# Linear attention into a mixture of four experts: another opening, and a bank of its own for the last product

## The chip, the cores and the metric

The kernel runs on one core of a Trainium2 chip. The metric is device time in microseconds, the median of several executions. A second source is one profiled execution, whose trace gives start and duration of every instruction.

## The reference

Two stages, B = 8 batches, H = 8 heads, S = 576 positions, 64 values per head, four experts:

```python
q_p, k_p = phi(q), phi(k)                 # phi(x) = where(x > 0, x, exp(x) - 1) + 1
kv  = einsum('bhsd,bhse->bhde', k_p, v)
z   = k_p.sum(axis=2)
x   = einsum('bhsd,bhde->bhse', q_p, kv) / (einsum('bhsd,bhd->bhs', q_p, z) + 1e-6)
x   = x.transpose(0, 2, 1, 3).reshape(4608, 512)
p   = domain_probs / domain_probs.sum(-1)
out = sum over e of  p[:, e] * (relu(x @ w1[e]) @ w2[e])     # w1: 512x1024, w2: 1024x512
```

## The kernel before

**Tiling.** The attention is done per batch and per pair of heads (four pairs). Of 576 positions, 512 are handled as four chunks of 128, and 64 are a rest. For each pair: phi of k and q (an exponent on ScalarE, ACT, and two operations on VectorE, DVE), a transpose of phi(q) on TensorE (PE), the products kv and z (PE, into PSUM), a copy of kv to SBUF (ACT), numerators and denominators (PE), the division (DVE: a reciprocal and a product). The experts follow on x. Batch 0 is done with plain matrix products (`first_l1`, L775, and `first_l2`, L822); of its 8 column blocks of expert 0, seven are held open at once in seven PSUM banks, so that their four slices of the contraction (dc) can be added as the four pairs of x become ready (L750). Later batches run in 64 units of two chunks and one expert, each with seven products of half size for w1 (`l1_seven`, L897) and seven for w2 (`l2_unit`, L978) in place of eight, with sums of weights (L715, L736) and of activations around them. Four PSUM banks l2b hold the second product over the four experts of a chunk pair.

**Order.** The order of the instructions is set by a planner (class `Plan`, L21): each step is added with an engine, a planned duration, a due time and keys that it reads and writes, and the planner lays them out; every engine then runs its list in that order. The list of POOL (GpSimd), which issues most of the loads up to 68 us, stays in the order in which the steps were added. Between planned steps of the first 21 us, PE runs extra matmuls whose result nobody reads (`keep_warm`, L1161).

**The opening.** `load_first` (L325) loads k, q or v of one pair of batch 0 (256 KB), `load_first_rest` (L333) the rest of k or v of one pair (32 KB), `load_w1` (L348) slices of w1 (512 KB, cast to 16 bits on the way). Before: SP issues k0, q0, k1, two rests of k, four rests of v, q1; ACT issues two rests of k; POOL waits for the landing of k0 (`hold="k0"`) and issues v0, k2, q2, v1, slice 0 of w1, k3, q3, v2, v3, the other slices of w1, and so on (L1090 to L1106, L1110). In `first_attention` (L474) the numerators and denominators of a pair lie side by side, 65 columns a head, two chunks in the bank `at` and two in l2b1 (L511); each half has its own reciprocal (L518) and product (L519); x is transposed (L528) and copied (L533) as the operand of the first product.

**The end.** In the last unit (`end`, L1006) DVE adds up the seven products as they are finished, six additions (L1053), and the result is stored in four parts: the second half of each row block after the fourth addition, the first half after the sixth, one part from SP and one from ACT each time (L1055).

Of the kernel before, what the change touches and what calls it, by code (L numbers as in the profile page):

```python
# [137 lines left out]
def kernel(  # L138
# [16 lines left out]
    P = 128  # L155
# [92 lines left out]
        A["t", 2, i] = [("ek", 2 + i, 0), ("ek", 2 + i, 1)]  # L248
    A["t", 2, 2], A["w1x", 2, 0] = [("k_r", g) for g in range(DC)] + ["v_r", "kp_r"], ["ek_r"] + [("v_r32", g) for g in range(DC)]
    ones = sb("ones", [P, 2, 1], FP16)  # L250
    rc4 = sb("rc4", [P, 2, C], FP32)
    xt0 = s4_b[1].rearrange("p a c t -> p a (c t)")
    hts = [h_b[i][:, t, f].rearrange("p c t -> p (c t)") for i in range(2)
           for t in range(2) for f in range(2)]
# [75 lines left out]
        dma(queue, pri, o, t[0, 2 * pr : 2 * pr + 2, 0:NT].rearrange("h (p c) d -> p h c d", c=C),  # L330
            (key,), 0.72, hold=hold, mark=mark)

    def load_first_rest(t, o, queue, pri, key, g):  # L333

        n = 2 * R // DC
        dma(queue, pri, o[g * n : (g + 1) * n].rearrange("p h t d -> p h (t d)"),
            t[0, 2 * g : 2 * g + 2, NT:S].rearrange("h (p t) d -> p h (t d)", t=2),
            ((key, g),), 0.17)

    def load_rest(b, queue, pri, after=0.0, parts=(0, 1, 2)):  # L340
        par = b % 2
# [132 lines left out]
    def first_attention(pr, pri, step):  # L474
# [3 lines left out]
        fs = slice(pr * P, (pr + 1) * P)  # L478
        g = slice(pr * 2 * R // DC, (pr + 1) * 2 * R // DC)
        ni = pr % 2  # L480
        nds = [bank[:, 0 : C * DE].rearrange("p (c h e) -> p c h e", c=2, h=2)
               for bank in (at, l2b[1])]
        kv3 = l2b[2][:, 0 : 2 * DE].rearrange("p (h e) -> p h e", h=2)
        tq = tbank[:, 0:NT]
        last = pr == DC - 1
# [22 lines left out]
            nc.scalar.copy(kvz[0:D, 0, :], kv3[0:D, 0, :])  # L508
            nc.scalar.copy(kvz[D:P, 1, :], kv3[D:P, 1, :])

        def nd(u):  # L511
            for c in range(2):
                nc.tensor.matmul(out=nds[u][:, c], lhsT=qT[:, 2 * u + c], rhs=kvz,
                                 start=True, stop=True)

        def norm(u):
            rc = rc4[:, u].rearrange("p (c h e) -> p c h e", c=2, e=1)
            nc.vector.reciprocal(rc, nds[u][:, :, :, D:DE])  # L518
            nc.vector.tensor_tensor(  # L519
                out=x_b[0][:, 2 * u : 2 * u + 2, fs].rearrange("p c (h d) -> p c h d", h=2),  # L520
                in0=nds[u][:, :, :, 0:D],
                in1=rc.broadcast_to([P, 2, 2, D]),
                op=AO.mult,
            )

# [17 lines left out]
        pl.add("PE", 0.5, pri + 4 * step, kv,  # L543
               r=(("kqp", pr, 0), ("v_o", pr), "v_r", "kp_r"), w=("l2b2",))
        pl.add("ACT", 0.45, pri + 4.5 * step, kvcopy, r=("l2b2",), w=(("kvz", pr),))
        for u in range(2):
            pl.add("PE", 0.12, pri + (5 + 0.1 * u) * step, lambda u=u: nd(u),
                   r=(("qT", ni), ("kvz", pr)), w=(("at", "l2b1")[u],))
            pl.add("DVE", 0.63, pri + (5.5 + 0.1 * u) * step, lambda u=u: norm(u),
                   r=(("at", "l2b1")[u],), w=(("xk", pr, u),))  # L550
        bk = ("l1b2", "l2b3" if last else "l1b2")
        xw = ("s4", 1, pr)
        for u in range(2):
# [221 lines left out]
    def first_l1(e, pri, step, nb):  # L775
        ht = []
        banks = [(l1b[i], "l1b%d" % i) for i in range(3)]
        if nb > 3:
            banks[2:] = [(l2b[0], "l2b0"), (l2b[2], "l2b2"), (at, "at"), (l2b[1], "l2b1")]
            banks += [(l1b[2], "l1b2")]  # L780
        ht = [rot("ht", len(hts)) for _ in range(FC)]

        def relu(fj, bank, key, pr_):
            if nb > 3 and fj in RELU:
                pl.add("DVE", 0.62, pr_, lambda: nc.vector.tensor_scalar(
                    hts[ht[fj]], bank, 0.0, None, AO.max), r=(key,), w=(HTK[ht[fj]],))
                return
            pl.add("ACT", 0.5, pr_, lambda: nc.scalar.activation(hts[ht[fj]], bank, AF.Relu),
                   r=(key,), w=(HTK[ht[fj]],))

        done = 0
        if nb:
            b0 = cnt.get("l1", 0) if nb < 4 else 0
            late = lambda fj: LATE if fj > 2 else 0.0
# [183 lines left out]
    def l2_unit(n):  # L978
# [5 lines left out]
        KW = lambda i, j_: k2(e, i, j_)  # L984
        T = lambda i: (("t", e, i),)

        def prod(bank, half, a, w, opens):
            for c in range(HF):
                nc.tensor.matmul(  # L989
                    out=l2b[bank][:, half * HD : (half + 1) * HD],  # L990
                    lhsT=a[:, c, :],
                    rhs=w[:, c],
                    start=(opens and first and c == 0),
                    stop=(last and c == HF - 1),
                    skip_group_check=True,
                )

# [8 lines left out]
        end = n == nu - 1  # L1006
        if first:
            seq = (P1, P5, P2, P6, P7, P4, P3)
        elif end:
# [2 lines left out]
        for i, (bank, half, a, ak, w, wk, opens) in enumerate(seq):  # L1012
            pl.add("PE", 0.436, p0 + 0.9 * i,
                   lambda bank=bank, half=half, a=a, w=w, opens=opens: prod(bank, half, a, w, opens),
                   r=(ak,) + wk, w=lk(bank) + ((("p", bank, half),) if end else ()))
        if not last:
            return
        oi = rot("ot", 2)
# [20 lines left out]
        if end:  # L1039
            lo, hi = (lambda bank: l2b[bank][:, 0:HD]), (lambda bank: l2b[bank][:, HD : 2 * HD])  # L1040
            for dur, o, a_, b_, r, w in (
                (0.4, of[:, 0], hi(1), s15[:, 0], (("p", 1, 1), "s15"), (O(0),)),
                (0.4, of[:, 1], hi(0), of[:, 0], (("p", 0, 1),), (O(0),)),
                (0.62, of[:, 2:4], lo(3)[:, None].broadcast_to([P, 2, HD]), of[:, 0:2],
                 (("p", 3, 0), O(0)), (O(2),)),
                (0.4, of[:, 2], hi(2), of[:, 2], (("p", 2, 1),), (O(2),)),
                (0.4, of[:, 0], lo(1), s15[:, 0], ("l2b1",), (O(0),)),
                (0.4, of[:, 1], lo(2), of[:, 1], lk(2), (O(0),)),
            ):
                i = cnt.get("lp", 0)  # L1050
                cnt["lp"] = i + 1
                pl.add("DVE", dur, p0 + 2 + i * 0.5,
                       lambda o=o, a_=a_, b_=b_: tt(out=o, in0=a_, in1=b_, op=AO.add), r=r, w=w)  # L1053
                if i in (3, 5):
                    for par, queue in enumerate(("SP", "ACT")):  # L1055
                        store(int(i == 3), par, queue, (O(2 if i == 3 else 0),))
            return
        pl.add("DVE", 0.62, p0 + 4.5, lambda: tt(
# [16 lines left out]
    def consts(i):  # L1075
# [11 lines left out]
    nc.vector.memset(qTr[0], 0.0)  # L1087
    pl.add("DVE", 0.27, 36, lambda: nc.vector.memset(qTr[1], 0.0),
           w=[("qTr", 1, pr) for pr in range(DC)])
    load_first("SP", -9, k, 0, mark="k0")  # L1090
    load_first("SP", -8, q, 0)
    load_first("SP", -7, k, 1)
    for g in range(DC):
        load_first_rest(k, k_r, "ACT" if g < 2 else "SP", -6, "k_r", g)
    for g in range(DC):
        load_first_rest(v, v_r32, "SP", -4, "v_r32", g)
    load_first("SP", -3, q, 1)
    load_first("POOL", 0, v, 0, hold="k0")
    for pr in (2, 3):
        load_first("POOL", 0, k, pr)  # L1100
        load_first("POOL", 0, q, pr)
        if pr == 2:
            load_first("POOL", 0, v, 1)
            load_w1(0, (0,))
    load_first("POOL", 0, v, 2)
    load_first("POOL", 0, v, 3)  # L1106
    first_rest()
    for pr in range(DC):
# [49 lines left out]
                rest_maps(b, False, t - 2)  # L1158
            attention(b, pr, False, t, 1.5)

    def keep_warm(bank):  # L1161

        nc.tensor.matmul(out=bank[:, 256:512], lhsT=identh,
                         rhs=qTr[0][:, 0:2].rearrange("p a t -> p (a t)"), start=True, stop=True)

    prep(0)
# [11 lines left out]
    with tc.manual_schedule(  # L1178
# [7 lines left out]
    ):  # L1186
        todo = pl.order()
        free = 0.0
        warm, bank = True, l2b[0]
        for o in todo:  # L1190
            warm = warm and not (o["start"] > WARM or "l2b2" in o["w"] and bank is l2b[2] and o["dur"] < 0.3)
            bank = l2b[2] if "l2b0" in o["w"] else bank
            if o["eng"] == "PE" and warm:
                gap = o["start"] - free
                for _ in range(int((gap - 0.25) / 0.115) - (COLD if free == 0.0 else 0)):
                    keep_warm(bank)
                free = o["start"] + o["dur"]
            o["fn"]()

# [29 lines left out]
```

## Time and profile before

| | us |
|---|---|
| median of 4 runs (496.61 to 497.09) | 496.78 |
| profiled execution, device time | 497.0 |
| its span, first to last instruction | 495.2 |
| first L750 (first product of batch 0) starts | 15.37 |
| first L761 (second product of batch 0) starts | 24.80 |
| last matmul ends | 489.6 |
| last of the four last stores lands | 493.8 |

How to read the lines shown further on. The page's first part gives each engine's busy time, its share of the span and its number of instructions; PEld is the loading of weights into PE. A line of the waits has the engine and line that waited, what ended the wait, and total, count and longest in us. A line of the chain has start, duration, engine and what it did; it is the sequence of steps that ended last. A line of the timeline has start and duration (us), engine, line, operation, output and inputs, shape, count, and in brackets the idle time before it and what ended it. SPq, ACTq and POOL with DMA_DIRECT2D are issues of transfers. The DMA view gives the busy share of the 16 DMA engines in tenths and GB/s, in 40 equal slices of its window.

### The profile page before, as it was taken

What the parts mean: (1) busy time and instruction counts of PE and PEld (TensorE: products, weight loads), DVE (VectorE), ACT (ScalarE), POOL (GpSimd) and SP (SyncE); (2) the same over time, 40 slices, a digit from 0 to 9 for tenths busy, and PEclk for the clock granted to TensorE, in tenths of its full rate; (3) what the DMA queues carried; (4) which work ended last, traced back from release to release, by engine and by line L of the source; (5) the groups of instructions that cost most, each with busy time, mean ns of one, the idle gap of its engine ahead of it and who ended that gap; (6) DMA issues with size and microseconds to landing.
All of it is one profiled execution on the core that took longest, in us unless ns stands there. A gap on an engine that the chain in (4) does not pass through costs nothing.

```text
span 495.2 us, 14994 instructions
## 1 busy us (share of the span) xinstructions
PE 484.9 (98%) x6092; PEld 429.9 (87%) x6092; DVE 413.2 (83%) x1045; ACT 364.8 (74%) x686; POOL 41.2 (8%) x66
## 2 busy tenths in 40 slices
PE   7999999999999999999999999999999999999995
PEld 6544557999999999999999999999999999999994
DVE  6798999999998989899989899899987676767664
ACT  5636678978977898769876997699766767676641
POOL 7656600000000000000000000000000000000000
PEclk9999999999999999999999999999999999999998
DMA  8999968946765775878557655655623232323311
GB/s 218 215 233 220 269 140 227 216 88 177 113 164 127 163 157 132 159 159 151 126 128 164 133 151 125 181 126 127 152 54 87 45 87 44 88 44 86 46 44 42
DMA packets 125541, 66.98 MB, mean 135 GB/s; under 512 B 94592, under 2 KB 119696, under 8 KB 125472
## 3 DMA queue, kind: packets, MB, share of 16 engines
q1 hardware_dynamic: 115808, 51.99, 47.2%
q0 software_dynamic: 9344, 13.71, 13.6%
q8 instruction: 47, 0.77, 0.6%
q10 hardware_dynamic: 320, 0.33, 0.2%
q14 instruction: 22, 0.18, 0.1%
HBM read 45.16 MB, written 9.44 MB: 110 GB/s over the span
## 4 chain that ended last, share of the span: by engine, by line
PE 90%; DVE 3%; DMA 3%; ACT 1%; POOL 1%; issue 1%; DVEq 0%; ACTq 0%
PE l1b L913 40%; PE l2b L989 39%; PE l1b L750 4%; PE l2b L761 3%; PE at L653 2%; PE at L629 1%; DMA t<-in_v_dram 1%; DMA xT<-xp 1%; DVE t L736 1%; DMA kq<-in_k_dram 1%; DVE w1x L715 1%; POOL w1x L290 1%; DVE ot L826 1%; ACT xp L873 0%; PE l2b L750 0%
## 5 line engine op out<-in xcount | busy, mean ns | idle before, releaser
L913 PEld LDWEIGHTS <-w 128*128 128x128 f16 x2048 | 134.0, 98 | 5.3
L927 ACT ACTIVATE h<-l1b 128x512 f16<-128x512 f32 x128 | 76.7, 599 | 52.4 <-PE l1b L913 49.9
L989 PE MATMUL l2b<-w,h 128*128 128x256 f16 x768 | 115.0, 273 | 0.0
L989 PE MATMUL l2b<-t,s 128*128 128x256 f16 x768 | 114.6, 273 | 0.0
L913 PEld LDWEIGHTS <-w1x 128*128 128x128 f16 x1536 | 100.2, 98 | 4.1 <-issue 0.6
L989 PEld LDWEIGHTS <-s 128*128 128x128 f16 x1024 | 90.3, 98 | 6.3
L933 DVE CUSTOM_DVE_ANT_0 h<-l1b,p 128x512 f16<-128x512 f32 x64 | 44.2, 690 | 44.2 <-PE l1b L913 41.6
L873 ACT ACTIVATE xp<-x,p_nat 128x512 f16<-128x512 f16 x112 | 77.3, 721 | 2.3 <-DMA xT<-xp 1.9
L913 PE MATMUL l1b<-xs,w1x 128*128 128x128 f16 x1024 | 78.1, 219 | 0.1
L913 PE MATMUL l1b<-xs,w 128*128 128x128 f16 x1024 | 78.0, 219 | 0.0
L913 PE MATMUL l1b<-xT,w 128*128 128x128 f16 x1024 | 78.0, 219 | 0.0
L989 PEld LDWEIGHTS <-h 128*128 128x128 f16 x768 | 67.3, 98 | 4.5
L975 DVE TENSOR_TENSOR s<-h 128x512 f16<-128x512 f16 x128 | 53.9, 421 | 2.1
L930 ACT COPY l1b<-l1b 128x512 f32<-128x512 f32 x64 | 36.8, 574 | 12.0 <-PE l1b L913 11.4
L930 ACT COPY u<-l1b 128x512 f32<-128x512 f32 x64 | 37.5, 585 | 10.8 <-PE l1b L913 10.4
L933 DVE CUSTOM_DVE_ANT_0 h<-l1b,u 128x512 f16<-128x512 f32 x64 | 43.8, 685 | 1.3 <-PE l1b L913 0.2
L930 ACT COPY p<-l1b 128x512 f32<-128x512 f32 x64 | 37.4, 584 | 8.6 <-PE l1b L913 7.6
L891 DVE TENSOR_TENSOR xs<-xT,xs 128x256 f16<-128x256 f16 x128 | 36.9, 288 | 3.5
L913 PE MATMUL l1b<-xT,w1x 128*128 128x128 f16 x512 | 39.0, 219 | 0.0
L989 PE MATMUL l2b<-w,s 128*128 128x256 f16 x256 | 38.4, 273 | 0.0
L594 ACT ACTIVATE ek<-kq 128x512 f16<-128x512 f32 x54 | 33.9, 629 | 2.8 <-DMA kq<-in_k_dram 1.9
L975 DVE TENSOR_TENSOR s<-s,h 128x512 f16<-128x512 f16 x64 | 27.1, 424 | 5.6
(155 smaller groups left out, 579.8 us busy)
## 6 DMA issues: line engine op xcount, KB each, us to landing
w<-in_moe_w_dram POOLq DMA_DIRECT2D x32, 256.0 KB, 8.0
out_dram<-ot SPq DMA_DIRECT2D x16, 512.0 KB, 3.1
kq<-in_k_dram SPq DMA_DIRECT2D x26, 256.0 KB, 3.5
kq<-in_q_dram SPq DMA_DIRECT2D x26, 256.0 KB, 3.4
vs<-in_v_dram SPq DMA_DIRECT2D x24, 256.0 KB, 3.8
xT<-xp SPq DMA_TRANSPOSE x64, 3.1
kq<-in_k_dram POOLq DMA_DIRECT2D x3, 256.0 KB, 7.1
vs<-in_v_dram POOLq DMA_DIRECT2D x3, 256.0 KB, 7.1
```

The source lines that it names most:

```text
L594: pl.add("ACT", 0.55, pri + i * step, lambda i=i: nc.scalar.activation(ek[:, i], kq[:, i], AF.Exp), r=(sk[i],), w=(("ek", ei, i),))
L653: nc.tensor.matmul(out=slot[c - c0], lhsT=qT[:, c] if c < C else qTr[par][:, pr], rhs=kvz, start=True, stop=True,)
L750: nc.tensor.matmul(out=bank[:, ts], lhsT=w1_sb[e][:, dc, fj * P : (fj + 1) * P], rhs=xt0[:, dc, ts], start=(dc == 0), stop=(dc == DC - 1 a ...
L761: nc.tensor.matmul(out=bank, lhsT=hts[ht[fj]][:, c * P : (c + 1) * P], rhs=w2_sb[e][:, fj, :], start=(fj == 0), stop=(fj == FC - 1),)
L873: pl.add("ACT", 0.6, pri, lambda c=c, src=src, ps=ps: nc.scalar.activation(xp[:, c, :], src, AF.Copy, scale=ps), r=r, w=(("xp", xi, c),))
L891: lambda o=o, a=a, b_=b_: tt(out=o, in0=a, in1=b_, op=AO.subtract),
L913: nc.tensor.matmul(out=bank[:, fc * P : (fc + 1) * P], lhsT=wt[:, kc, fc * P : (fc + 1) * P], rhs=r[:, kc, :], start=(start and fc == 0 an ...
L927: return lambda: nc.scalar.activation(o, bank, AF.Relu)
L930: return lambda: nc.scalar.copy(o, bank)
L933: return lambda: nc.vector._custom_dve(TENSOR_ADD_SAT, out=o, in0=bank, in1=t, s0=BIG, s1=0.0)
L975: pl.add("DVE", 0.36, U(n + 1) + d - 0.5, lambda i=i, a=a, b_=b_, alu=alu: tt(out=s4[:, i], in0=a, in1=b_, op=alu), r=r, w=(Q(i),))
L989: nc.tensor.matmul(out=l2b[bank][:, half * HD : (half + 1) * HD], lhsT=a[:, c, :], rhs=w[:, c], start=(opens and first and c == 0), stop=( ...
```

## The change

Five edits.

1. *Loads.* SP issues k0, q0, k1, q1 and then the rests of v. ACT issues all four rests of k, the first of which is now what POOL's first load waits for. POOL issues v0, k2, q2, v1, k3, q3, v2, slice 0 of w1, v3, then as before.
2. *Numerators.* A pair's numerators for all four chunks go to one bank (`at` for even pairs, l2b1 for odd ones), its denominators to l2b0, by a matmul of 2 columns each; one reciprocal takes all eight denominators. The product is one operation for a pair; the last pair keeps two.
3. *Banks of the first product.* l2b0 changes its place with l2b2 among the seven banks, and the third block (`fj` = 2) gets the later due time too.
4. *The extra matmuls* write to l1b1 until its first use.
5. *The last product* (P3 of the last unit) goes to the free one of the three l1b banks. The fourth addition takes both halves of l2b2 at once, the sixth reads the l1b bank. Of the two stores after the fourth addition, one moves from ACT to POOL.

```diff
-        for u in range(2):
-            pl.add("PE", 0.12, pri + (5 + 0.1 * u) * step, lambda u=u: nd(u),
-                   r=(("qT", ni), ("kvz", pr)), w=(("at", "l2b1")[u],))
-            pl.add("DVE", 0.63, pri + (5.5 + 0.1 * u) * step, lambda u=u: norm(u),
-                   r=(("at", "l2b1")[u],), w=(("xk", pr, u),))
+        pl.add("PE", 0.36, pri + 5 * step, nd, r=(("qT", ni), ("kvz", pr)), w=(nk, "l2b0"))
+        pl.add("DVE", 0.22, pri + 5.4 * step, lambda: nc.vector.reciprocal(rc, den),
+               r=("l2b0",), w=(("rc4", pr),))
+        if last:
+            for u in range(2):
+                pl.add("DVE", 0.43, pri + (5.5 + 0.1 * u) * step,
+                       lambda u=u: norm(slice(2 * u, 2 * u + 2)),
+                       r=(nk, ("rc4", pr)), w=(("xk", pr, u),))
+        else:
+            pl.add("DVE", 0.7, pri + 5.5 * step, lambda: norm(slice(0, C)),
+                   r=(nk, ("rc4", pr)), w=(("xk", pr, 0), ("xk", pr, 1)))
...
+        def nd():
+            for c in range(C):
+                nc.tensor.matmul(out=num[:, c], lhsT=qT[:, c], rhs=kvz[:, :, 0:D],
                                  start=True, stop=True)
+                nc.tensor.matmul(out=den[:, c], lhsT=qT[:, c], rhs=kvz[:, :, D:DE],
+                                 start=True, stop=True)
...
-            banks[2:] = [(l2b[0], "l2b0"), (l2b[2], "l2b2"), (at, "at"), (l2b[1], "l2b1")]
+            banks[2:] = [(l2b[2], "l2b2"), (at, "at"), (l2b[0], "l2b0"), (l2b[1], "l2b1")]
...
+            own = end and (bank, half) == (2, 0)
+            out_ = l1b[free][:, 0:HD] if own else l2b[bank][:, half * HD : (half + 1) * HD]
...
-                (0.4, of[:, 2], hi(2), of[:, 2], (("p", 2, 1),), (O(2),)),
+                (0.62, of[:, 1:3], v2(l2b[2]), of[:, 1:3], (("p", 2, 1),), (O(0), O(2))),
                 (0.4, of[:, 0], lo(1), s15[:, 0], ("l2b1",), (O(0),)),
-                (0.4, of[:, 1], lo(2), of[:, 1], lk(2), (O(0),)),
+                (0.4, of[:, 1], l1b[free][:, 0:HD], of[:, 1], ("l1b%d" % free,), (O(0),)),
...
-                    for par, queue in enumerate(("SP", "ACT")):
+                    for par, queue in enumerate(("SP", "POOL" if i == 3 else "ACT")):
...
-    load_first("SP", -9, k, 0, mark="k0")
-    load_first("SP", -8, q, 0)
-    load_first("SP", -7, k, 1)
+    for pr in range(2):
+        load_first("SP", -9 + pr, k, pr)
+        load_first("SP", -9 + pr, q, pr)
     for g in range(DC):
-        load_first_rest(k, k_r, "ACT" if g < 2 else "SP", -6, "k_r", g)
+        load_first_rest(k, k_r, "ACT", -9, "k_r", g, mark=None if g else "go")
     for g in range(DC):
         load_first_rest(v, v_r32, "SP", -4, "v_r32", g)
-    load_first("SP", -3, q, 1)
-    load_first("POOL", 0, v, 0, hold="k0")
-    for pr in (2, 3):
-        load_first("POOL", 0, k, pr)
-        load_first("POOL", 0, q, pr)
-        if pr == 2:
-            load_first("POOL", 0, v, 1)
-            load_w1(0, (0,))
+    load_first("POOL", 0, v, 0, hold="go")
+    load_first("POOL", 0, k, 2)
+    load_first("POOL", 0, q, 2)
+    load_first("POOL", 0, v, 1)
+    load_first("POOL", 0, k, 3)
+    load_first("POOL", 0, q, 3)
     load_first("POOL", 0, v, 2)
+    load_w1(0, (0,))
     load_first("POOL", 0, v, 3)
```

The planner lays out all steps anew, so the order of steps of other engines changes in places up to the end, above all where attention steps of later batches stand among the units; the matmuls themselves stay the same.

More of the change, by code (lines that the diff above doesn't have):

```diff
@@ L250 @@
     ones = sb("ones", [P, 2, 1], FP16)
-    rc4 = sb("rc4", [P, 2, C], FP32)
+    rc4 = sb("rc4", [P, DC, 2 * C], FP32)
     xt0 = s4_b[1].rearrange("p a c t -> p a (c t)")
@@ L331, in load_first, with load_first_rest @@
             (key,), 0.72, hold=hold, mark=mark)
-    def load_first_rest(t, o, queue, pri, key, g):
+    def load_first_rest(t, o, queue, pri, key, g, mark=None):
         n = 2 * R // DC
@@ L337, in load_first_rest @@
             t[0, 2 * g : 2 * g + 2, NT:S].rearrange("h (p t) d -> p h (t d)", t=2),
-            ((key, g),), 0.17)
+            ((key, g),), 0.17, mark=mark)
     def load_rest(b, queue, pri, after=0.0, parts=(0, 1, 2)):
@@ L480, in first_attention @@
         ni = pr % 2
-        nds = [bank[:, 0 : C * DE].rearrange("p (c h e) -> p c h e", c=2, h=2)
-               for bank in (at, l2b[1])]
+        num, nk = ((at, "at"), (l2b[1], "l2b1"))[ni]
+        num = num.rearrange("p (c h d) -> p c h d", c=C, h=2)
+        den = l2b[0][:, 0 : 2 * C].rearrange("p (c h e) -> p c h e", h=2, e=1)
+        rc = rc4[:, pr].rearrange("p (c h e) -> p c h e", h=2, e=1)
         kv3 = l2b[2][:, 0 : 2 * DE].rearrange("p (h e) -> p h e", h=2)
@@ L509, in kvcopy, with norm @@
             nc.scalar.copy(kvz[D:P, 1, :], kv3[D:P, 1, :])
-        def nd(u):
-            for c in range(2):
-                nc.tensor.matmul(out=nds[u][:, c], lhsT=qT[:, 2 * u + c], rhs=kvz,
+        def nd():
+            for c in range(C):
+                nc.tensor.matmul(out=num[:, c], lhsT=qT[:, c], rhs=kvz[:, :, 0:D],
                                  start=True, stop=True)
-        def norm(u):
-            rc = rc4[:, u].rearrange("p (c h e) -> p c h e", c=2, e=1)
-            nc.vector.reciprocal(rc, nds[u][:, :, :, D:DE])
+                nc.tensor.matmul(out=den[:, c], lhsT=qT[:, c], rhs=kvz[:, :, D:DE],
+                                 start=True, stop=True)
+        def norm(cs):
             nc.vector.tensor_tensor(
-                out=x_b[0][:, 2 * u : 2 * u + 2, fs].rearrange("p c (h d) -> p c h d", h=2),
-                in0=nds[u][:, :, :, 0:D],
-                in1=rc.broadcast_to([P, 2, 2, D]),
+                out=x_b[0][:, cs, fs].rearrange("p c (h d) -> p c h d", h=2),
+                in0=num[:, cs],
+                in1=rc[:, cs].broadcast_to([P, cs.stop - cs.start, 2, D]),
                 op=AO.mult,
@@ L793, in first_l1 @@
             b0 = cnt.get("l1", 0) if nb < 4 else 0
-            late = lambda fj: LATE if fj > 2 else 0.0
+            late = lambda fj: LATE if fj > 1 else 0.0
             for dc, u in [(dc, 2) for dc in range(DC - 1)] + [(DC - 1, 0), (DC - 1, 1)]:
@@ L985, in l2_unit @@
         T = lambda i: (("t", e, i),)
+        free = cnt["l1u"][0]
+        end = n == nu - 1
         def prod(bank, half, a, w, opens):
+            own = end and (bank, half) == (2, 0)
+            out_ = l1b[free][:, 0:HD] if own else l2b[bank][:, half * HD : (half + 1) * HD]
             for c in range(HF):
                 nc.tensor.matmul(
-                    out=l2b[bank][:, half * HD : (half + 1) * HD],
+                    out=out_,
                     lhsT=a[:, c, :],
                     rhs=w[:, c],
-                    start=(opens and first and c == 0),
-                    stop=(last and c == HF - 1),
+                    start=(((opens and first) or own) and c == 0),
+                    stop=((last or n == nu - 2) and c == HF - 1),
                     skip_group_check=True,
@@ L1005, in l2_unit @@
         seq = (P1, P4, P5, P2, P6, P7, P3)
-        end = n == nu - 1
         if first:
@@ L1014, in l2_unit @@
                    lambda bank=bank, half=half, a=a, w=w, opens=opens: prod(bank, half, a, w, opens),
-                   r=(ak,) + wk, w=lk(bank) + ((("p", bank, half),) if end else ()))
+                   r=(ak,) + wk,
+                   w=(("l1b%d" % free,) if end and i == 6 else lk(bank)) + ((("p", bank, half),) if end else ()))
         if not last:
@@ L1159, in batch, with keep_warm @@
             attention(b, pr, False, t, 1.5)
-    def keep_warm(bank):
-        nc.tensor.matmul(out=bank[:, 256:512], lhsT=identh,
+    def keep_warm():
+        nc.tensor.matmul(out=l1b[1][:, 256:512], lhsT=identh,
                          rhs=qTr[0][:, 0:2].rearrange("p a t -> p (a t)"), start=True, stop=True)
@@ L1188 @@
         free = 0.0
-        warm, bank = True, l2b[0]
+        warm = True
         for o in todo:
-            warm = warm and not (o["start"] > WARM or "l2b2" in o["w"] and bank is l2b[2] and o["dur"] < 0.3)
-            bank = l2b[2] if "l2b0" in o["w"] else bank
+            warm = warm and o["start"] < WARM and "l1b1" not in o["w"]
             if o["eng"] == "PE" and warm:
@@ L1195 @@
                 for _ in range(int((gap - 0.25) / 0.115) - (COLD if free == 0.0 else 0)):
-                    keep_warm(bank)
+                    keep_warm()
                 free = o["start"] + o["dur"]
```

## The prediction

> Lines are those of the kernel before. "dc" is one of the four slices of the contraction in the first product of batch 0; its matmuls are L750, and L761 is the second product.
>
> **What bounds it now.** I read the busy table first, then the waits of TensorE (PE) from 24.8 us on, then the chain of waits of the first 80 us.
>
> ```profile
> PE 484.9 (98%) x6092; PEld 429.9 (87%) x6092; DVE 413.2 (83%) x1045; ACT 364.8 (74%) x686; POOL 41.2 (8%) x66
> ```
> ```profile
> PE at L632 <- DVE kqpr L402: 0.6, 1, 0.6
> ```
> The second line is the whole answer for 24.8 to 495 us: one wait of 0.6 us in 470. So from the first L761 on, PE is a full pipe, and the change takes no matmul out of it. The time can move in two places only: when that pipe starts, and what follows its last matmul. The start is in the chain and in PE's timeline:
>
> ```profile
> 0.74 3.22 DMA kq<-in_k_dram
> 3.96 0.30 issue
> 4.25 0.84 POOL w1x L290
> ...
> 9.25 5.32 DMA t<-in_v_dram
> ...
> 14.61 0.71 PE l2b L504 x12
> ```
> ```profile
> 11.29 0.27 PE L513 MATMUL at<-kvz,qT 128*128 128x130 f16 x2 [0.39 <-ACT kvz L509]
> ...
> 15.37 0.38 PE L750 MATMUL l1b<-s,w 128*128 128x512 f16 x1
> ...
> 24.80 7.07 PE L761 MATMUL l2b<-w,h 128*128 128x512 f16 x32
> ```
> The chain is a queue of loads: POOL may issue only when the first k has landed (3.96), then issues one load each 0.7 us, and v of pair 2 (issued 9.25, landed 14.57) lets PE go on. After 15.37 PE has 9.43 us of work and small waits until L761.
>
> **Part 1: POOL's loads start earlier.** They now wait for the first rest of k, issued by ACT at 0.75; the trace has it landed 2.4 us later, 3.2. With the same 0.3 us of issue, POOL starts at 3.5 instead of 4.25: 0.8 us earlier. ACT issues four small loads instead of two (0.91 us for two, so it ends at 2.6) and then loads its table (1.28 us, to 3.9); the first k lands at 3.96, which covers it by less than 0.1 us. SP loses two rests of k (0.94 us) and issues q of pair 1 at 2.3 instead of 5.13. The DMA view of the first 10 us, in slices of 0.25, shows what room there is:
>
> ```profile
> DMA  0000000132999999999996363799699999899999
> GB/s 0 0 0 0 0 0 0 61 51 61 320 379 359 375 373 340 287 303 309 342 248 154 78 62 41 86 172 156 131 262 381 402 463 369 320 393 371 234 205 223
> ```
> From 5.0 to 7.2 us the engines move 40 to 250 GB/s, before and after that 300 to 460. The 256 KB of q1 (0.7 us at 370 GB/s) move out of the full stretch behind 7.2 into this hole. So the loads on POOL land between 0.8 and 0.8 + 0.7 = 1.5 us earlier; I take 1.3, since little else can use the hole.
>
> **Part 2: their order.** Landings are issue plus time to landing, from the answers on L290. One slice of w1 takes 1.4 us between landings (11.2 to 12.6), k, q or v 0.6 to 0.7. The slice moves behind k3, q3, v2. Landings, before and forecast: k3 13.4, 10.7; q3 14.0, 11.3; v2 14.6, 11.9; w1 slice 0 12.7, 13.3; v3 15.2, 13.9; w1 slice 3 19.4, 18.1.
>
> **Part 3: from q1 to the first L750.** ACT's order is now: both exponents of pairs 0 and 1, rest of k, copy of qT0, copy of v's rest (ends 9.0, as before), exponents of pair 2, copy of kv0. Before, it waited 0.78 us here, for k2 until 9.77; k2 should land at 8.5. Two exponents at a pitch of 0.53 and the copies of 0.41 put kv0's copy at 10.5 and its numerators (L513) at 10.6: 0.7 earlier. PE is ready: turn 7.62, eleven warm-up matmuls at 0.11 to 9.05, turn 0.22, kv 0.6, so 9.9. ACT then has no wait: qT1 0.48, two exponents 1.06, kv1 0.46, qT2 0.48, copy of x of pair 0 0.58; from 10.55 that is 13.6. The first L750 starts at 13.65, its slice of w1 is there at 13.3. Before: 15.37.
>
> **Part 4: new norm.** A pair had two times reciprocal and product, 1.10 us of DVE in all:
>
> ```profile
> 11.64 0.18 DVE L518 RECIPROCAL rc<-at 128x4 f32<-128x4 f32 x1
> 11.85 0.42 DVE L519 TENSOR_TENSOR x<-at,rc 128x256 f16<-128x256 f32 x1
> 12.20 0.17 DVE L518 RECIPROCAL rc<-l2b 128x4 f32<-128x4 f32 x1
> 12.40 0.42 DVE L519 TENSOR_TENSOR x<-l2b,rc 128x256 f16<-128x256 f32 x1
> ```
> Now it has one reciprocal (0.21 with its gap) and one product of 128x512, which L785 shows as 0.69 from PSUM, 0.6 as a pitch: 0.85, so 0.25 saved. x of pair 0 is ready at 12.0 and transposed at 12.4, ahead of its copy at 13.0: the saving lies beside ACT's queue, and I cost it at nothing; without that cover it would be worth 0.25. PE pays: per pair four matmuls of 130 columns (0.057 each) become eight. L504 shows such pairs, 128 columns and then 2, at 0.055 + 0.03, so 0.34 instead of 0.23. All pairs share one bank of denominators: a pair's L513 waits for the reciprocal before it, which forecasts put 0.5 us ahead or more.
>
> **Part 5: to the first L761.** After 13.65 PE has 32 L750 at 0.216 = 6.91, two numerators 0.68, kv3 0.55, turn 0.22, three transposes of x 0.66: 9.02. Waits: the last numerators for kv3's copy 0.4, a transpose for a copy 0.1. The same account for before gives 6.91 + 1.89 + 0.45 = 9.25 against 9.43, so 0.2 is missing; I add it. 13.65 + 9.02 + 0.5 + 0.2 = 23.37, against 24.80: **1.4 us earlier.**
>
> **Part 6: does it carry to the end?** What PE needs afterwards must be early as well. w2 slice 0: 20.7 to 19.4, wanted at 23.4. Slice 3 of expert 1's w1: 29.9 to 28.6, wanted at 30.3. The rest of v of batch 1: copied at 42.1, wanted at 43.1; it moves 1.3 against 1.4. VectorE (DVE) is the tight one: the product of L459 ends at 37.57 and PE's L451 starts at 37.62, so it has no slack there. But in the new order eleven of the twelve sums of weights (0.65 each) stand ahead of that product, and the last relu ahead of them no longer waits behind a sum. It gains 1.4 + 0.65. I cost this part at zero.
>
> **Part 7: the end.** The third product's sum moves to an idle bank, and DVE's fourth addition goes from 128x256 (0.42) to 128x512 (0.69, the form of the third), so what follows is 0.27 later.
>
> ```profile
> 488.42 1.75 DVE L1053 TENSOR_TENSOR ot<-l2b,ot 128x256 f32<-128x256 f32 x3
> 490.09 0.41 DVE L1053 TENSOR_TENSOR ot<-l2b,s 128x256 f32<-128x256 f32 x1
> 490.42 0.41 DVE L1053 TENSOR_TENSOR ot<-l2b,ot 128x256 f32<-128x256 f32 x1
> ```
> ```profile
> 490.20 1.39 ACTq L290 DMA_DIRECT2D out_dram<-ot  x2
> ```
> PE's last matmul ends at 489.6, so DVE, not PE, ends the work. Its fourth addition starts at 489.74, right behind the third, which ends at 489.64: a bank of its own buys at most 0.1. The last store now goes out at 491.15 instead of 490.86, but it is ACT's only one (2.6 us to landing, the second took 2.9): 493.8, as before. The store moved to POOL is issued at 490.5; SP's landed in 2.3 us, POOL's first load of 256 KB in 4.1. So it lands between 492.8 and 494.6: 0 to 0.8 us on the end. I take 0.1, near SP's row, since POOL's was twice as large and shared the engines.
>
> Two pages speak here. The Trainium skill's "DMA: Bandwidth & Descriptors", Specifications, gives POOL's path about 0.4 us more to the first byte than SP's and ACT's; estimated by that page, the moved store lands at 493.2 and adds nothing, while POOL's own row would add 0.8. The skill's "PSUM — Partial Sum Buffer", on bank collisions, wants TensorE and VectorE kept out of one bank altogether, disjoint columns too; by that rule the fourth addition had to wait for the last product, and the trace leaves no more than that 0.1 for it.
>
> **Sum.** -1.4 + 0.1 = -1.3 us. The profiled execution took 497.0 (span 495.2), 0.2 over the median of 496.78: 495.7 for it, **495.5** for the median.
>
> **Rivals.**
> - *The opening gains a third.* The engines are so full that POOL's stream lands as before. Then slice 0 of w1, now behind v2, comes at 14.6, and 14.6 + 9.7 = 24.3 at L761: 0.5 earlier, 496.4. For it: 300 to 400 GB/s from 7.2 on. Against it: the hole.
> - *Given back.* PE arrives 1.4 earlier and meets something with a margin of about 1 us (rest of v, DVE at L451), or POOL's store takes the full 4.1 us: 0.5 to 0.9 back, 496.2.
> - *q1 late: slower.* Its exponent moved from eighth in ACT's order to fourth, ahead of everything that feeds kv0. It may land at 7.0 for nothing (qT0's copy can't start before 8.1); beyond, each us is a us. At 8.3 the gain is gone; in before it landed at 9.0 while it shared the engines with POOL, though issued at 5.13; at 9.5 the kernel takes 496.8 - 1.3 + 2.5 = 498.0. Against it: SP has moved k0, q0 and k1 by 5.8, so q1 has 0.2 MB left when POOL's packets begin. I expect 6.6 to 7.0.
>
> **Numbers.** Forecast 0.60, gain of a third 0.15, given back 0.12, q1 late 0.13 (0.10 beyond +0.2%). A measurement of this kernel can tell about 0.2% (1 us) from no change: faster 0.60, same 0.30, slower 0.10. Range: at best the stream gains 1.5 and the waits of 0.5 go, -2.0, 494.8; to the other side it takes in both middle cases and q1 up to 8.9, 497.4.
>
> **What would show it.** POOL's first load at 3.5; q1 landed by 7.0; first L750 near 13.7 and first L761 near 23.4; PE without waits after that, except the 0.6 at L632; DVE's last addition 1.5 us after PE's last matmul instead of 1.2; POOL's store not the last to land. Wrong if L761 starts after 24, if PE waits anew between 30 and 80 us, or if the span beyond PE's last matmul grows by over 0.5.

## The result and the profile after

The changed kernel takes **498.12 us** (median of 35 executions, 497.29 to 500.02); the kernel before, on the same chips, 496.89 (53 executions). The ratio is 1.0022, 95% interval 1.0017 to 1.0028: **slower by 1.1 us (0.85 to 1.4)**, where 1.3 less was forecast. (The ratio is close to that of the means; the medians differ by 1.2.) The profiled execution of the changed kernel took 498.4, span 496.6 (before: 497.0 and 495.2).

A caution for all that follows: single executions of one kernel lie up to 1.9 us to either side of its median, and a profile shows one of them. So sizes come from the ratios, and places from the profiles.

**The middle** first, as in the prediction: the busy table, then the waits of PE from 20 us on.

```profile
PE 484.0 (97%) x6105; PEld 429.7 (87%) x6105; DVE 412.2 (83%) x1038; ACT 365.0 (74%) x686; POOL 41.4 (8%) x67
```
```profile
PE at L661 <- DVE x L674: 0.2, 1, 0.2
```
PE is still a full pipe; the 0.6 at L632 went, 0.2 at L661 came. It has 13 matmuls more: sixteen small ones of the new numerators, less three of the extra ones. From the first L769 to its last matmul PE takes 464.3 us, against 464.8 before; the five runs below that keep PE's old order (e2, e3, e8, e9, e10) have 464.0 to 466.0. So the loss is not in the middle.

**The opening.** The chain of the first 18 us begins with ACT's first rest of k (landed 3.00) and goes on through POOL's loads to slice 3 of w1; POOL starts at 3.30, 0.95 earlier than before. PE's timeline and ACT's show what came of it (columns as before: start, duration, engine, line; in brackets the idle time and what ended it).

```profile
0.74 2.27 DMA t<-in_k_dram
3.00 0.30 issue
3.30 0.84 POOL w1x L290
...
10.94 7.37 DMA w<-in_moe_w_dram
```
```profile
9.28 0.38 PE L497 MATMUL l2b<-s,kqp 128*128 128x128 f16 x4 [1.00 <-ACT qT L543]
...
10.45 0.21 PE L506 MATMUL l2b<-t 32*128 32x128 f16 x1 [0.47 <-ACT t L426]
...
14.89 0.38 PE L758 MATMUL l1b<-s,w 128*128 128x512 f16 x1
...
24.44 0.81 PE L769 MATMUL l2b<-w,h 128*128 128x512 f16 x3
```
```profile
6.89 0.63 ACT L538 ACTIVATE ek<-kq 128x512 f16<-128x512 f32 x1 [1.52 <-DMA kq<-in_k_dram]
...
9.99 0.41 ACT L426 CAST t<-w1x 128x256 f16<-128x256 f32 x1 [0.76 <-DMA w1x<-in_v_dram]
```
The first product (L758, formerly L750) starts 0.48 earlier and the second (L769, formerly L761) 0.36; forecast were 1.7 and 1.4. ACT stands twice: for k1 until 6.87 (landed at 5.80 before) and for the last rest of v until 9.89 (7.73 before). The DMA view of the first 10 us, beside that of the prediction, has no hole between 5.0 and 7.2 us any more:

```profile
DMA  0000000312999999999999999999999989999999
GB/s 0 0 0 0 0 0 0 66 45 90 332 367 354 369 365 371 318 307 309 299 367 283 316 287 193 217 359 397 371 256 422 274 285 176 211 318 373 399 334 434
```

**The end.** DVE's timeline: two additions of 128x512 (the third and the now wider fourth), the fifth, the sixth, and POOL's store.

```profile
488.08 1.49 DVE L1066 TENSOR_TENSOR ot<-l2b,ot 128x512 f32<-128x512 f32 x2
...
489.48 0.41 DVE L1066 TENSOR_TENSOR ot<-l2b,s 128x256 f32<-128x256 f32 x1
...
489.81 0.41 DVE L1066 TENSOR_TENSOR ot<-l1b,ot 128x256 f32<-128x256 f32 x1
489.86 0.56 POOL L290 DMA_DIRECT2D out_dram<-ot  x1 [426.72 <-DVE ot L1066]
```
PE's last matmul ends at 488.74, 0.87 earlier than before, but what follows takes 7.9 us instead of 5.6. Two views lead to the reason. The chain's last piece is an instruction of POOL's sequencer; the chain counts it only to 490.42, where POOL's issue of the store ends. The view of that line gives its kind and its whole length (minimum, median and maximum duration in ns, then first and last start):

```profile
489.84 0.58 POOLq L1235
```
```profile
L1235 POOLq DRAIN  x3: 51/93/6015, 489.8 to 496.4; - x3
...
L1235 ACTq EVENT_SEMAPHORE  x2: 17/17/17, 496.0 to 496.6; - x2
```
The DRAIN is an instruction at the end of POOL's list. It begins with the issue of POOL's last transfer, at 489.84, and lasts to 495.85, 2.5 us past the landing of that store (493.32), while the last of the other stores has landed at 493.87. The other engines' closing semaphores, of which ACT's are shown, come right behind it, from 496.0. In the kernel before the same instruction took 8.4 us, from 62.03 to 2.5 us past the landing of POOL's last load (67.98), where nobody waited for it:

```profile
L1224 POOLq DRAIN  x3: 51/102/8441, 62.0 to 494.7; - x3
```
Also, the stores behind the first land later: 3.3 to 3.6 us after issue, where SP's took 2.3 and ACT's 2.6 and 2.9 before.

### The profile page after: what moved, and what is told of

The parts are those of the page before. It is cut to its first block, busy times and chain, and to the rows that moved or that the text cites. A ratio compares the mean times of both kernels' runs of the same rounds, so it can differ in the third digit from the quotient of the medians.

```text
span 496.6 us, 15022 instructions
## 1 busy us (share of the span) xinstructions
PE 484.0 (97%) x6105; PEld 429.7 (87%) x6105; DVE 412.2 (83%) x1038; ACT 365.0 (74%) x686; POOL 41.4 (8%) x67
## 4 chain that ended last, share of the span: by engine, by line
issue 86%; DMA 9%; POOL 2%; ACT 1%; DVE 1%; POOLq 0%; DVEq 0%; ACTq 0%
DMA w<-in_moe_w_dram 6%; DMA kq<-in_q_dram 2%; POOL w L290 1%; POOL w1x L290 1%; DMA t<-in_k_dram 0%; DVE w1x L723 0%; POOL t L290 0%; POOL xp L290 0%; POOL prawr L290 0%; ACT h L796 0%; POOL xr_sb L290 0%; POOL kq L290 0%; ACT ek L602 0%; ACT ek L406 0%; POOLq L1235 0%
## 5 line engine op out<-in xcount | busy, mean ns | idle before, releaser
L938 ACT COPY u<-l1b 128x512 f32<-128x512 f32 x64 | 37.5, 586 | 10.6 <-PE l1b L921 10.5
```

Source lines behind the costliest of these rows:

```text
L938: return lambda: nc.scalar.copy(o, bank)
```

## The experiments

Differences "against before" are ratio minus 1, times 496.9 us, with their 95% interval; each was measured beside the kernel before. Where the end is "the old one", the last unit's product, its additions and its stores are those of the kernel before.

### The end

**e1: the moved store back on ACT.**
```diff
-for par, queue in enumerate(("SP", "POOL" if i == 3 else "ACT")):
+for par, queue in enumerate(("SP", "ACT")):
```


> The changed kernel with the moved store back on ACT (all four last stores from SP and ACT). Theory (the drain): POOL's last DRAIN ended 2.5 us after its store had landed and 1.5 us after the other engines were done; without a late store of POOL it ends near 70 us as in the kernel before, and the others land in 2.3 to 2.9 us after issue as there, not in 3.3 to 3.6. Span 496.6 - 2.0 = 494.6, time about 0.6 us below the kernel before. Rival (the store only crowded the other stores): the landings come 0.5 earlier and no more, span 496.1, time about 0.9 above the kernel before.

Measured: +0.05 against before (-0.5 to +0.6), span 494.6; so the store on POOL is 1.05 of the change's 1.1 (about 0.4 to 1.7 by the two intervals). In the profiles what follows PE's last matmul shrinks from 7.9 to 6.2, and the drain, which outlasted SP's part of the closing by 1.5, is nearly all of it. The span met the theory by luck, since PE's last matmul ends 0.4 earlier in this execution; the median did not meet it, and the other stores still take up to 3.5 to land (DMA to landing, us, of the four stores):
```profile
DMA to landing us min/median/max: 2.3/3.1/3.5
```
The later landings do not come from POOL, then.

**e2: the kernel before, that one store on POOL. e3: the kernel before, an earlier store (at 471 us) on POOL.** One line each, as above.

> The kernel before with one edit alone: the second of the two stores after the fourth addition goes out from POOL instead of ACT. Theory (the drain): span +1.3 to +1.9 (the store lands at about 493.8, the drain ends at 496.3, where all was done at 494.2). Rival (a late landing only): it lands by 494.6 at the latest, so at most +0.4.

> The kernel before with one earlier store of the last batch (64x512, issued at about 471 us) moved from SP to POOL; the last four stay. Theory (the drain follows the last transfer of POOL by 2.5 us): it ends near 477, nobody waits for it, time as before within 0.2 us. Rival (any store by POOL late in the kernel costs, by waking its queue or by what is done at the end of the program for a queue used again): +1 us or more.

Measured: e2 +1.9 (+1.2 to +2.5), e3 +0.4 (-0.15 to +0.95). The DRAIN in e2 (first) and e3:
```profile
L1224 POOLq DRAIN  x3: 51/93/5622, 490.0 to 496.1; - x3
```
```profile
L1224 POOLq DRAIN  x3: 51/93/5622, 471.2 to 494.9; - x3
```
It took 5.62 us both times, and ended 2.6 us (e2) and 3.1 us (e3) behind the store's landing. In e2 it ends at 495.60, where the last store has landed at 493.44. In e3 it is over at 476.8, over 18 us before the end. POOL's store itself landed in 2.96 and 2.50 us, where SP's beside it took 2.3 to 2.7. Behind PE's last matmul e2 takes 7.45 us and e3 5.7. The price is the place in the program, not the transfer. e3's interval leaves room for up to 1 us, but not through the drain.

**e8: the kernel before with the own bank and the wider addition alone.** The order of every engine's instructions is that of the kernel before.

> The kernel before with the last product in its own bank and the wider fourth addition, all stores from SP and ACT as before: nothing else differs. By the row of the wider addition (0.69 instead of 0.42, DVE has no slack behind PE's last matmul) +0.3. By the run with the changed opening and this end, whose span behind PE's last matmul was 6.3 where the kernel before has 5.6 (the last two stores took 3.2 and 3.5 to land instead of 2.4 and 2.9): +0.6. If the bank of its own pays (no wait on the bank that the last product writes): level or below.

Measured: +0.85 (+0.3 to +1.35), and the last three stores took 3.1 to 3.5 again. The DMA view of 488 to 495 us shows one transfer more than that of the kernel before, by its queue:
```profile
q1 hardware_dynamic: 160, 0.26, 14.8%
q10 hardware_dynamic: 160, 0.26, 10.8%
q14 instruction: 1, 0.01, 0.3%
```
By the name of its queue it is an instruction fetch: one packet of 8 KB and 0.31 us, 2.4 us after the first of these stores is issued. In the kernel before it comes at 495.5, when all is done. The trace has 1346 instructions of DVE, its sequencer's included, where the kernel before, e2, e3 and e4 have 1345. That gave a theory which has nothing to do with banks: the number of DVE's instructions sets when the fetch comes.

**e9: the kernel before with one DVE instruction more. e10: e8 with one less.**
```diff
 nc.vector.memset(qTr[0], 0.0)
+nc.vector.memset(ones, 1.0 / SX)          # e9
...
-nc.vector.memset(ones, 1.0 / SX)          # e10
+nc.gpsimd.memset(ones, 1.0 / SX)
```


> The kernel before with one more instruction on DVE (the small memset of ones at the start is done twice); the end is untouched. In three profiles with the product's own bank, DVE has 1346 instructions instead of 1345, and an instruction fetch of 8 KB falls among the last stores (2.0 to 2.4 us after the first of them is issued), where it comes behind the end in the others; the stores then land in 3.1, 3.2 and 3.5 instead of 2.6, 2.4 and 2.9. Theory (the count of DVE's instructions sets when that block is fetched, and the fetch delays the stores): the same here, last landing 0.5 to 0.6 later, time +0.5. Rival (the late landings belong to the own bank and the wider addition): landings as before, time within 0.1.

> The kernel before with the own bank and the wider addition, stores from SP and ACT, and one DVE instruction less (the memset of ones goes to POOL, which is idle then). Theory (fetch): no fetch among the last stores, they land in 2.3 to 2.9 again; what is left of the own bank is its wider addition, +0.27. Rival: landings of 3.1 to 3.5 and +0.8 as with 1346 instructions.

Measured: e9 +0.7 (+0.25 to +1.15), e10 +0.4 (-0.05 to +0.85). The landings, e9 first:
```profile
DMA to landing us min/median/max: 2.3/3.1/3.5
```
```profile
DMA to landing us min/median/max: 2.3/2.5/2.9
```
A memset of 0.06 us at the start of the kernel, 490 us away, moves the landing of the last stores by 0.6; with one instruction less, the landings are those of the kernel before although the own bank is there. The rival is out. How one packet of 0.31 us makes the last landing 0.6 later is not shown. Behind PE's last matmul e9 takes 5.98 us, e8 6.23 and e10 5.88, where the kernel before takes 5.61. What is left of the own bank in e10 fits its wider addition (0.27), within a wide interval.

**e11: e1 with one DVE instruction less** (the second pair of lines above).

> The changed kernel with the last stores from SP and ACT alone and one DVE instruction less (the memset of ones goes to POOL). Theory (drain and fetch together explain the end): the span behind PE's last matmul goes from 6.2 (stores from SP and ACT alone) to 5.65 + 0.27 = 5.9, time 0.3 below the kernel before, 0.4 to 0.5 below the same kernel with 1346 instructions. Rival: no change against that one, level with the kernel before.

Measured: -0.25 (-0.75 to +0.25); landings 2.3 to 2.9, 5.8 us from PE's last matmul to the end of the span (6.2 in e1). The intervals of e11 and e1 overlap; the landings do not.

### The opening

**e4: the new opening, the old end** (e1 with the last product, its additions and keys as before).

> The changed kernel's opening alone: the last unit, its additions and its stores as in the kernel before. If the opening with the waits of PE behind it gave 0.87 us (PE's last matmul 488.47 against 489.34) and the end cost all the rest, the span is 495.2 - 0.9 = 494.3, the time 0.9 below the kernel before; the run with the store back on ACT should be 0.2 to 0.3 above it (the wider fourth addition). If the opening gained nothing that lasts, it is level with the kernel before.

Measured: **-0.55** (-0.95 to -0.1). Its profiled execution was the slowest of its twelve. With e11, e1 and the change itself this makes a ladder: -0.55, then -0.25 (own bank and wider addition), +0.05 (fetch), +1.1 (store on POOL). The opening gains 0.55, the end costs 1.65 (about 1.1 to 2.1). The intervals of the first three overlap; of the steps alone, only the store's is clear of noise. The stretch behind PE's last matmul, which scatters less, has the same steps: 5.6 us in e4 (5.2 to 5.7 in the eleven profiles with the old end, the last stores from SP and ACT and no fetch among them), 5.85 in e11, 6.24 in e1, 7.89 in the change.

**e5: e4 with POOL held on k0 again.**
```diff
-load_first_rest(k, k_r, "ACT", -9, "k_r", g, mark=None if g else "go")
+load_first_rest(k, k_r, "ACT", -9, "k_r", g)        # and mark="go" on k0
```


> The changed opening with the old end, and POOL's first load held again on the landing of the first k instead of the first rest of k. Theory (POOL's early packets take the engines from k1, q1 and the rests of v, which ACT's order needs): k1 lands near 5.8 instead of 6.6 to 6.9, the last rest of v near 8.5 instead of 9.2 to 9.9, ACT's first numerators are up to 0.5 earlier; POOL's stream lands 0.3 to 0.8 later. First L769 within 0.5 of the 24.4 to 24.5 of the early start, so the early start bought little. Rival (the landings of k1 and of the rests of v depend on what SP and ACT have queued themselves): they land as late as with the early start, and all behind POOL comes 0.8 later: first L769 at 25.1 to 25.3, +0.7 on the time.

Measured: +0.55 (+0.05 to +1.0), 1.1 above e4; first L769 at 25.15; k1 at 6.46, the last rest of v at 8.61. My theory fell for k1, and in the time the rival was right: POOL's early start is worth about 1 us (about 0.5 to 1.7), of which 0.6 to 0.8 is there at the first L769. With the old loads (seven profiles) k1 lands at 5.7 to 6.0, with the new ones (all others but e13, e15 and e16, eight profiles) at 5.9 to 6.9, early POOL or not.

**e6: the new norm and banks with the old loads. e12: the new loads with the old norm and banks.** Edits 2 to 4 alone, and edit 1 alone.

> The kernel before's loads and the old end, with the new norm and the new banks alone. Theory (norm lies beside ACT's queue): time as before within 0.3, first second product of batch 0 at 24.8 within 0.3. Rival (the norm is what the opening gained, since loads gained nothing by the landings): 0.5 below the kernel before, and level with the changed opening.

> The kernel before with the change's loads alone: order of SP's, ACT's and POOL's loads and what POOL's first waits for; norm, banks, extra matmuls and the end as before. The new norm and banks alone came out at +0.6, the whole new opening at -0.55. If the parts add up: -1.15, about 495.6, below every kernel so far, with the first second product of batch 0 about 24.0. Rival (the two need each other, the loads only pay with one norm for a pair; or the planner's new order decides): level with the whole new opening or above it, -0.5 to +0.5.

Measured: e6 +0.6 (+0.1 to +1.05), e12 -0.2 (-0.65 to +0.2). Neither theory for e6 got its size. For e12 the rival held: the parts do not add up (-0.2 + 0.6 against -0.55). Each of these kernels gets an order of its own from the planner, also behind the opening. In e6's profile the second product starts early, at 24.26, but PE waits 0.9 for a relu of ACT there, and the stretch from its start to the start of the last L769 is 54.2 us, against 53.1 in the kernel before. But this is e6's fastest execution, and e9, with the old order, has 54.2 too. So +0.6 is the price of edits 2 to 4 with their order, and where it arises is not shown. In e12's profile the second product starts at 23.54, the earliest of all, 0.9 ahead of the change's: an early start there is not yet a gain in time.

**e7 and e14: slice 0 of w1 earlier,** behind v1 (e7) or behind q3 (e14), else as e4. In e1 and e4 the first product had waited for that slice, here e1:
```profile
PE l1b L758 <- DMA w<-in_moe_w_dram: 0.6, 1, 0.6
```


> The changed opening with the old end, and slice 0 of w1 in its old place behind v1. In two of the profiles with the new order the first product of batch 0 waited 0.6 for that slice (landed 14.8 to 14.9). Theory (after the early start slice 0 is the last to come): with the old place it lands near 12.2, the first product starts 0.5 earlier at 14.3, but k3, q3 and v2 come 1.3 later, and kv of pairs 2 and 3 wait for them; net within 0.4 of the new order. Rival (the order is the opening's whole gain): first product after 15.2, 0.5 above the new order.

> The changed opening with the old end, and slice 0 of w1 one place earlier, between q3 and v2. Rival B (slice 0 is the limit): it lands 0.6 earlier, near 13.2, the first product starts 0.4 to 0.6 earlier, v2 comes 1.3 later but is wanted only by the third pair; time 0.3 to 0.5 below the changed opening. Theory A (ACT's order is the limit): first product as before at 14.4 to 14.9, and the later v2 costs up to 0.5.

Measured: e7 -0.05 (-0.75 to +0.65), e14 **-0.85** (-1.35 to -0.4). Both lost that wait. In e7 the first product started at 14.45, near the theory, and the second at 23.82, but from there to the last L769 it took 55.3 us (52.8 to 54.6 in all other profiles), and PE waited anew for ACT's relus:
```profile
PE l1b L758 <- ACT h L796: 1.7, 2, 1.1
```
In e14's profile the 0.6 for the slice became 0.8 for v2:
```profile
PE l2b L506 <- DMA t<-in_v_dram: 0.8, 1, 0.8
```
and the first product started at 14.93, as in e4: in time rival B was right, in place theory A. So its profile does not show where its 0.3 against e4 comes from, and the two intervals overlap.

**e13, e15, e16: the rests of v ahead of q1** (on e4, on e14, and on e12).
```diff
...
 load_first("SP", -8, k, 1)
-load_first("SP", -8, q, 1)
...
 for g in range(DC):
     load_first_rest(v, v_r32, "SP", -4, "v_r32", g)
+load_first("SP", -3, q, 1)
```


> The changed opening with the old end, and the four rests of v ahead of q1 on SP, as in the kernel before. In five profiles with the change's loads the last rest of v landed at 9.0 to 9.9 (7.1 to 7.7 with the old loads), and ACT's copy of them stands ahead of everything that feeds the first numerators. Theory A (k1 and the rests of v hold ACT up): they land 7.5 to 8.3, q1 near 8.8, the first numerators and with them the first product of batch 0 come 0.5 to 0.8 earlier, time 0.3 to 0.8 below the changed opening (0.55 below the kernel before), about -1.0. Rival B (slice 0 of w1, landed at 13.5 to 14.9, is what the first product waits for): the first product stays at 14.4 to 14.9, no gain.

> Both: rests of v ahead of q1, and slice 0 between q3 and v2. If each limit stands right behind the other (A and B both): the first product near 13.7 and the first second product near 23.5, as the forecast had them, time 0.8 to 1.3 below the kernel before, more than either alone. If it is given back after 24 us by a new order of ACT's relus (as the run with slice 0 behind v1 had it, first second product at 23.8 and PE's last matmul at 490.0): no gain in time although the first second product is early.

> The kernel before with the change's loads alone, but the rests of v ahead of q1; norm, banks and end as before. Theory A: 0.3 to 0.8 below the loads alone (which came out 0.2 below the kernel before), so -0.5 to -1.0. Rival B: level with the loads alone.

Measured: e13 +0.35 (-0.3 to +1.0), e15 -0.2 (-0.85 to +0.4), e16 +0.1 (-0.45 to +0.65): no gain from any, each 0.3 to 0.9 above the kernel that it is built on. ACT's timeline in e13 (the slowest execution of its twelve, so by its place, not its size):
```profile
7.91 0.40 ACT L426 CAST t<-w1x 128x256 f16<-128x256 f32 x1 [0.68 <-DMA w1x<-in_v_dram]
...
10.95 0.63 ACT L538 ACTIVATE ek<-kq 128x512 f16<-128x512 f32 x1 [2.15 <-DMA kq<-in_q_dram]
```
The rests of v land at 7.75 as theory A wanted, and q1, issued at 4.87, lands at 10.92 (10.5 in e16; 11.3 in e15, whose profile is its slowest execution too), ahead of kv0's copy in ACT's order. In these runs whatever SP issues last pays. That its packets share the engines with POOL's stream is the likely reason, not a tested one. The Trainium skill, "DMA: Bandwidth & Descriptors", Queues, rings and completion order, says that a DMA engine goes round its queues packet by packet; the landings agree with such sharing, and no run here shows the turn itself.

## Why the prediction was wrong

- **What bounds it:** right. PE stayed full from the second product on, and what the runs can price lies at the two ends. Two of the forecast's signs of being wrong came: the second product starts at 24.44, after 24, and the span beyond PE's last matmul grew by 2.3, not under 0.5.
- **Part 1, POOL's start:** right in its sign: POOL started at 3.30 (forecast 3.5), and e5 prices the early start at about 1 us. But "little else can use the hole" gave the hole to q1, and POOL's own packets filled the rest: from 5.0 to 7.2 us SP's queue moved 0.37 MB (0.17 before) and POOL's 0.30 (0.10 before). q1 landed at 7.80, not 6.6 to 7.0.
- **Part 2, the stream:** in the changed kernel's profile 0.4 to 0.7 behind the forecast for k3 to slice 0 of w1. In four profiles of the new opening (the change, e1, e4, e11) v2 landed at 13.1 and slice 0 at 14.4 in the mean, 1.1 to 1.2 behind it.
- **Part 3, the failing step of the opening:** "copy of v's rest (ends 9.0, as before)". SP's loads were moved past each other, and I followed only q1. The rests of v stand behind q1 now and land at 9.0 to 9.9; their copy ends at 10.4, and the first numerators run at 11.82, not at 10.6 (11.29 before). The first L758 at 14.89, not 13.65.
- **Part 4, the norm:** costed at nothing; alone, with its banks and order, it was +0.6 (e6); within the new loads no cost shows (-0.55 in e4, -0.2 in e12). From the first operation to the end of the last it took 0.94, against 1.18 in the four rows of before: 0.24 saved, where 0.25 was forecast (the terms named there, 0.21 and 0.6, give 0.81 and not 0.85):

```profile
12.33 0.21 DVE L549 RECIPROCAL rc<-l2b 128x8 f32<-128x8 f32 x1
12.58 0.69 DVE L521 TENSOR_TENSOR x<-at,rc 128x512 f16<-128x512 f32 x1
```
- **Parts 5 and 6:** from the first to the second product it took 9.55, where Part 5 had 9.72, so what failed is the start in Part 3. 1.4 for the opening came out as 0.55 (0.1 to 0.95); in the mean of four and six profiles the second product of batch 0 starts at 24.3 with the new opening and 24.7 with the old. That this carries to the end was right for the change itself; e7, with the second product at 23.82 and no gain in time, shows that it need not.
- **Part 7, the failing step of the sum:** "I take 0.1". The wider addition was foreseen (DVE ends 1.49 after PE, forecast 1.5). The store on POOL was priced up to its landing, 0 to 0.8, and it did land ahead of ACT's. What follows a landing was not asked: POOL's DRAIN, visible at 62.0 to 70.5 in the trace of before, costs 1.05 (e1 against the change) to 1.9 (e2) when it begins at 490; in the profiles, 1.65 and 1.84. The fetch, some 0.3 (e1 against e11) to 0.7 (e9), was in no term.
- **The rivals:** the opening gaining a third was about right (0.5; 0.55 came, and slice 0 did come at 14.4 in the mean of four profiles; but in the change's own profile it came at 13.72 and nothing waited for it, so the size is in part luck), as was the worry about one late load of SP, only it was the rests of v and k1 as well as q1. No rival had a price behind the landing of POOL's store.

Open is how the missing 0.85 of the opening is divided between the rests of v, k1 and slice 0: the remedies tried for the rests of v and for slice 0 moved the wait to another load or to ACT's relus, and new orders by the planner may move the time by as much (e6). The lowest time of all runs is e14's, the changed opening with slice 0 behind q3 and the old end: ratio 0.9983 (0.9973 to 0.9992), 0.85 us below the kernel before and 1.9 below the change.

## What to carry to other kernels

At the end of a kernel, follow a transfer past its landing to the last instruction of the engine that issued it: an engine that has long finished its transfers looks free to use, and here one store gave it a closing wait of its own. When loads change queues, follow each load that an in-order engine waits for, not only the one that moved forward. And before a difference of half a microsecond at the end is put down to an edit, look whether an instruction fetch has moved.

## What was not expected of the hardware

- POOL's DRAIN ends 2.5 to 3.1 us after the landing of POOL's last transfer (2.6 in e2, 3.1 in e3, 2.5 in the sixteen other profiles). In e1 and e3 SP's wait for the last landing ends within 0.1 us of it.
- With 1346 instructions of DVE (e1, e8, e9, the change) an 8 KB instruction fetch falls among the last stores, of which all but the first land in 3.1, 3.2 and 3.5 us (3.5, 3.3 and 3.6 in the change) instead of 2.6, 2.4 and 2.9; with 1345 (the kernel before, e2 to e5, e10, e11, e16) it comes after the end, with 1354 (e12) 1.0 us before the first store, and the landings are short. The Trainium skill, "Runtime: NRT & Kernel Launch", Instruction fetch mechanics, has each sequencer fetch the next block ahead through a DMA queue of its own, in blocks of 16 KiB, mostly hidden. The queue of its own is in the DMA view, with 8 KB on this one; hidden it is not here, since the stores that land late with it are what the kernel waits for (e9: +0.7).
